# Attention steps of a fused attention, soft-MoE and FFN kernel: TensorE takes scores, values and router products together and then all transposes, and the copy of transposed x follows the exponential

## The chip, the cores and the metric

The kernel runs on one core of a Trainium2 chip. The metric is the device time of one execution in microseconds, lower is better. The engines are TensorE (PE in the rows, its weight loads PEld), VectorE (DVE), ScalarE (ACT), GpSimd (POOL) and SyncE (SP), which issues all the DMAs of this kernel.

## The reference

Three stages run one after the other: chunked attention with eight memory keys for each head, a soft mixture of experts, and a feed-forward block with a squared relu. Batch 4, 8 heads, 768 positions, head width 64; chunks of 32 queries see 16 keys to the left and 8 to the right.

```python
for c in range(nc):                                   # attention, 24 chunks of 32
    scores = scale * (q_c @ k_full.T)                 # k_full: 8 memory keys + up to 56 context keys
    a = exp(scores - max); a = a / (a.sum(-1) + 1e-9)
    out[:, :, c_start:c_end] = a @ v_full
x = out.transpose(0, 2, 1, 3).reshape(3072, 512)

logits = x @ phi                                      # soft MoE, 8 experts of 4 slots
d = softmax(logits, axis=0); slot_input = d.T @ x
slot_out[e] = relu(slot_input[e] @ w1[e]) @ w2[e]     # w1: 512 x 1024, w2: 1024 x 512
x = softmax(logits, axis=1) @ slot_out

h = relu(x @ w_in); out = (s * h * h + b) @ w_out     # FFN, 512 -> 2048 -> 512
```

## The kernel before

The attention is cut into 32 units (u = 0 to 31): four batches, two halves of 384 positions, four pairs of heads. Four units of one batch and half make a group g (0 to 7). A loop of 32 steps (s = 0 to 31) is a software pipeline written out by hand: each call in it is `when(unit, function)` or `at(s, k, function)`, and the order of the calls is the order of instructions on each engine, since nothing is rescheduled. The engines take their instructions in that order.

In step s the main work is this:

- `kspread(s+1)` on GpSimd spreads the keys of the next unit (lines L263 to L267).
- `emit_s(s)` on TensorE makes the scores (24 small matmuls, L285, and a mask, L288 or L290), into PSUM tile s. I write S(s).
- `soft_sum(s-1)`, `soft_max(s)`, `soft_eps(s-1)`, `soft_sub(s)`, `soft_rec(s-1)` on VectorE are the softmax's reductions, and `soft_exp(s)` on ScalarE is the exponential (L301).
- `emit_t(s-1)` transposes the exponentials on TensorE (L317, tile pt), and ScalarE copies them out of PSUM (L319). I write T(s-1).
- `emit_pv(s-2)` multiplies by the values (24 small matmuls, L325, tile x); VectorE evacuates and normalises them (`emit_xevac`, L331). I write PV(s-2).
- `emit_xt(s-3)` transposes the attention output on TensorE (L339, tile xt), and ScalarE copies that (L341 before, L344 in the changed file). I write xt(s-3).

Router work comes once for a group of four steps: `emit_lp` (L346, its copy `emit_g1` L351) in steps where s mod 4 is 3, `emit_g2` (L356, copy L358) and `emit_ln` (L362) where it is 0, `emit_g3` (L413, copy L414) where it is 1, and `emit_g4` (L419, slot inputs) where it is 2. After the loop an epilogue written out by hand drains the pipeline (units 30 and 31, group 7), and then come experts (L630 first weights, L668 second weights) and the FFN.

SyncE's queue takes the loads in program order. At the end of a step stand `load_qk(s+5)` (396 KB, into a ring of five buffers, free again after S of an older unit), in odd steps from 3 on `load_v(s+1)` (four DMAs of 192 KB, values of two units, into a ring of two buffers, free after PV of the older pair), and in odd steps one `load_w` (1 MB of expert weights). A DMA also waits for the DMA eight issues before it. After the loop the rest of the weights follow; where they reuse slots, they wait for the work on the old content.

Of the kernel before, what the change touches and what calls it, by code (L numbers as in the profile page):

```python
# [35 lines left out]
def kernel(  # L36
# [11 lines left out]
    nc = tc.nc  # L48
# [18 lines left out]
    def psum(tag, shape):  # L67
        bufs = {"s": 2, "g": 2}.get(tag, 1)
        return ps.tile(shape, F32, tag=tag, name=tag, bufs=bufs)
# [48 lines left out]
    with tc.manual_schedule():  # L118
# [27 lines left out]
        xts_r = Ring(p_r.end, 5, UT)  # L146
# [44 lines left out]
        def load_w(n, cap=None):  # L191
            for _ in range(n):
                i = wnext[0]
                if i < (len(order) if cap is None else cap):
                    src = srcs[order[i][0]][order[i][1]]
                    p = at_[order[i]] if i < npre else (16 + (i - npre) % NRG) * SLOT
                    if p is SPLIT:
                        wt[order[i]] = [area(x, SLOT // 2) for x in p]
                        for x in range(2):
                            nc.sync.dma_start(out=wt[order[i]][x], in_=src[:, SLOT // 2 * x:SLOT // 2 * (x + 1)])  # L200
                        wnext[0] += 1
                        continue
                    t = area(p, SLOT)
                    if order[i] == ("w2", W2 - 1):
                        wt[order[i]] = [t[:, SLOT // 2 * x:SLOT // 2 * (x + 1)] for x in range(2)]
                        for x in range(2):
                            nc.sync.dma_start(out=wt[order[i]][x], in_=src[:, SLOT // 2 * x:SLOT // 2 * (x + 1)])
                        wnext[0] += 1
                        continue
                    if src.dtype != F32:  # L210
                        t, src = t.bitcast(I32), src.bitcast(I32)
                    nc.sync.dma_start(out=t, in_=src)
                    wt[order[i]] = t
                    wnext[0] += 1
# [19 lines left out]
        def unit(u):  # L234
            g, hp = divmod(u, NHP)
            b, hf = divmod(g, HALF)
            return g, b, hf, hp
# [28 lines left out]
                                    in0=memk[:, b, hp].unsqueeze(2).to_broadcast([128, 2, NCU, NM]), **one)  # L266
            (nc.gpsimd if u else nc.vector).tensor_scalar(out=k[64:128, PAD + KL:], in0=k[64:128, PAD:PAD + UT], **one)  # L267

        s_t, x_t, gs = ({} for _ in range(3))

        def kwin(kt, c):
            a = kt[:, 32 * c:32 * c + KW]
# [38 lines left out]
        def soft_rec(u):  # L311
            nc.vector.reciprocal(out=r_r[u], in_=r_r[u])  # L312
# [8 lines left out]
        def emit_pv(u):  # L321
            xp = psum("s" if u == NU - 1 else "x", [128, NTU, 2, 64])
            for c in range(NCU):
                t, r = divmod(c, 4)
                nc.tensor.matmul(out=xp[32 * r:32 * r + 32, t], lhsT=pts_r[u][:, 32 * c:32 * c + 32],  # L325
                                 rhs=vbuf[u // 2 % 2][:, u % 2, :, 64 * c:64 * c + 64], start=True, stop=True)
            x_t[u] = xp

        def emit_xevac(u):
            g, b, hf, hp = unit(u)  # L330
            nc.vector.tensor_tensor(  # L331
                out=xs_r[g][:, :, 128 * hp:128 * hp + 128].rearrange("p t (h d) -> p t h d", h=2),
                in0=x_t.pop(u), in1=r_r[u].unsqueeze(3).to_broadcast([128, NTU, 2, 64]), op=ALU.mult)

        def emit_xt(u):
            g, b, hf, hp = unit(u)
            xt = psum("pt" if u == NU - 1 else "xt", [128, UT])
            for t in range(NTU):
                nc.tensor.transpose(out=xt[:, 128 * t:128 * t + 128],  # L339
                                    in_=xs_r[g][:, t, 128 * hp:128 * hp + 128], identity=ident)  # L340
            nc.scalar.copy(out=xts_r[u], in_=xt)  # L341

        def emit_lp(g):
            lp = psum("lp", [128, UT])  # L344
            for hp in range(NHP):
                nc.tensor.matmul(out=lp[32 * hp:32 * hp + 32, :], lhsT=phis[:, hp, :], rhs=xts_r[NHP * g + hp],  # L346
                                 start=True, stop=True)
            gs[g, "lp"] = lp
# [16 lines left out]
        def gsm(g):  # L365
            return [gsm_r[g][0:96, i:i + 1] for i in range(4)]
# [14 lines left out]
        def emit_ce(g):  # L381
            nc.scalar.activation(out=cs_r[g], in_=cs_r[g], func=AF.Exp)
# [7 lines left out]
        def emit_g2e(g):  # L390
            mo = mrun[(g + 1) % 2]
            gm, nmx, al, sg = gsm(g)
            nc.scalar.activation(out=eT_r[g][0:96], in_=lts_r[g][0:96], func=AF.Exp, bias=nmx,
                                 accum_out=lrun[0] if g == 0 else sg)
            if g:
                nc.scalar.activation(out=al, in_=mo, func=AF.Exp, bias=nmx)
            if g < NG - 1:
                emit_ce(g)
# [12 lines left out]
        def emit_g3(g):  # L411
            ep = psum("g", [128, NTU, NS])
            nc.tensor.transpose(out=ep.rearrange("p t s -> p (t s)"), in_=eT_r[g][0:96], identity=ident[0:96, 0:96])  # L413
            nc.scalar.copy(out=en_r[g], in_=ep)  # L414
# [36 lines left out]
        def at(s, k, *fns):  # L451
            if (s - k) % NHP == 0 and 0 <= (s - k) // NHP < NG:
                for fn in fns:
                    fn((s - k) // NHP)

        def when(u, fn):
            if 0 <= u < NU:
                fn(u)

        kspread(0)  # L460
        for s in range(NU):
            when(s + 1, kspread)
            at(s, 9, emit_g2e)
            when(s, emit_s)
            when(s - 1, soft_sum)
            when(s - 1, emit_t)
            at(s, 7, emit_lp)
            at(s, 8, emit_g2)
            at(s, 10, emit_g4)
            when(s, soft_max)  # L470
            when(s - 1, soft_eps)
            when(s, soft_sub)
            when(s, soft_exp)
            when(s - 1, soft_rec)
            at(s, 7, emit_g1)
            at(s, 10, emit_g4b)
            when(s - 2, emit_pv)
            at(s, 9, emit_g2b)
            when(s - 2, emit_xevac)
            at(s, 9, emit_g2c)  # L480
            at(s, 8, emit_ln)
            when(s - 3, emit_xt)
            at(s, 8, emit_g2a, emit_g2n)
            at(s, 9, emit_g3)
            when(s + NKB, load_qk)
            if s >= 3:
                when(s + 1, load_v)
            if s % 2 == 1:
                load_w(1, NWA)
            if s == NU - 2:  # L490
                load_w(1)
        load_w(19 - wnext[0])

        z, gl = NU - 1, NG - 1
# [29 lines left out]
        emit_xevac(z - 1)  # L524
        soft_rec(z)
        emit_xt(z - 2)
        emit_g2e(gl - 1)
        emit_pv(z)
        load_w(2)
        emit_xevac(z)  # L530
        emit_xt(z - 1)
        emit_xt(z)
        emit_g3(gl - 1)
        emit_lp(gl)
        load_w(1)
# [403 lines left out]
        for k in range(2):  # L939
# [3 lines left out]
                  in_=sot[:, k:k + 1, :, 0:4].to_broadcast([128, 4, 4, 4]))  # L943
# [151 lines left out]
```

## Time and profile before

| what | value |
|---|---|
| median of three runs | 471.84 us (471.58 to 471.96) |
| the profiled execution's own time | 473.56 us |
| its span | 471.8 us |
| PE busy | 453.8 us, 96% |
| PEld, DVE, ACT, POOL busy | 342.3, 309.8, 307.4, 84.2 us |
| DMA | 83.04 MB, mean 176 GB/s |

Busy time is summed over stages of different kinds: attention lasts until about 117 us of the span, the experts until about 167 us, and the rest is the FFN. A busy TensorE here is one whose matmuls, with modelled ends, overlap; it is not one at its peak. The DMA mean hides that nearly all loads fall in the first 172 us.

### The profile page before, as it was taken

What the parts mean: (1) busy time and instruction counts of PE and PEld (TensorE: products, weight loads), DVE (VectorE), ACT (ScalarE), POOL (GpSimd) and SP (SyncE); (2) the same over time, 40 slices, a digit from 0 to 9 for tenths busy, and PEclk for the clock granted to TensorE, in tenths of its full rate; (3) what the DMA queues carried; (4) which work ended last, traced back from release to release, by engine and by line L of the source; (5) the groups of instructions that cost most, each with busy time, mean ns of one, the idle gap of its engine ahead of it and who ended that gap; (6) DMA issues with size and microseconds to landing.
All of it is one profiled execution on the core that took longest, in us unless ns stands there. A gap on an engine that the chain in (4) does not pass through costs nothing.

```text
span 471.8 us, 10205 instructions
## 1 busy us (share of the span) xinstructions
PE 453.8 (96%) x3960; PEld 342.3 (73%) x3960; DVE 309.8 (66%) x685; ACT 307.4 (65%) x635; POOL 84.2 (18%) x154
## 2 busy tenths in 40 slices
PE   6898999899999989999999999999999999999996
PEld 5565767575555466878787888888888888888885
DVE  6677888876486879999495999976523224224232
ACT  4465766666224458898685988666666666666660
POOL 6665556541000000000000000007600000000000
PEclk8899999999999999999999999999999999999999
DMA  8999999999999952433422000004001001001011
GB/s 313 374 400 391 387 407 401 408 382 345 419 410 401 414 232 89 151 119 110 158 90 90 1 1 0 1 0 169 35 0 68 0 1 67 0 1 67 1 67 67
DMA packets 20576, 83.04 MB, mean 176 GB/s; under 512 B 2736, under 2 KB 2864, under 8 KB 14640
## 3 DMA queue, kind: packets, MB, share of 16 engines
q1 hardware_dynamic: 20528, 82.39, 45.1%
q8 instruction: 31, 0.51, 0.4%
q14 instruction: 17, 0.14, 0.1%
HBM read 76.09 MB, written 6.29 MB: 175 GB/s over the span
## 4 chain that ended last, share of the span: by engine, by line
PE 70%; DVE 11%; DMA 9%; ACT 3%; issue 2%; SPq 2%; POOL 1%; DVEq 0%; POOLq 0%; ACTq 0%
PE g L879 11%; PE xt L879 6%; PE x L879 6%; PE pt L879 5%; PE lp L879 5%; PE g L891 5%; DMA vals<-in_vm_dram 4%; PE s L827 4%; DMA seg<-in_w_dram 4%; PE x L325 3%; PE s L630 3%; PE xt L891 3%; PE x L891 3%; PE lp L891 3%; PE pt L891 3%
## 5 line engine op out<-in xcount | busy, mean ns | idle before, releaser
L844 DVE TENSOR_TENSOR glo<-r,ghi 128x384 fp32r<-128x384 f32 x128 | 76.5, 602 | 79.5 <-ACT ghi L841 79.3
L833 ACT ACTIVATE r<-s 128x384 f32<-128x384 f32 x128 | 62.7, 490 | 48.7 <-PE s L827 48.6
L837 ACT ACTIVATE r<-r 128x384 f32<-128x384 f32 x128 | 67.3, 526 | 9.6 <-DVE glo L844 5.4
L841 ACT CAST ghi<-r 128x384 fp32r<-128x384 f32 x128 | 65.4, 511 | 3.4
L827 PE MATMUL s<-cpack,mpack 128*128 128x384 f32 x128 | 44.3, 349 | 0.2 <-DVE mpack L820 0.2
L301 ACT ACTIVATE seg<-seg 128x384 f32<-128x384 f32 x32 | 28.7, 898 | 18.4 <-DVE seg L312 15.0
L879 PE MATMUL g<-whi,ghi 128*128 128x512 f32 x126 | 39.8, 395 | 0.2 <-DVE mpack L820 0.2
L891 PE MATMUL g<-wlo,ghi 128*128 128x512 f32 x128 | 39.7, 390 | 0.0
L879 PE MATMUL g<-whi,glo 128*128 128x512 f32 x126 | 39.3, 393 | 0.0
L866 POOL TENSOR_TENSOR keys<-keys,bias 128x512 f32<-128x512 f32 x6 | 8.4, 1428 | 162.6 <-DVE bias L855 162.6
L263 POOL TENSOR_SCALAR keys<-keys 64x416 f32<-64x416 f32 x63 | 33.6, 534 | 14.3 <-DMA keys<-in_kq_dram 9.0
L285 PE MATMUL s<-keys 128*32 128x128 f32 x768 | 30.1, 290 | 4.5 <-POOL keys L267 3.5
L325 PE MATMUL x<-vals,seg 128*32 128x128 f32 x744 | 28.5, 280 | 3.7 <-DMA vals<-in_vm_dram 2.9
L325 PEld LDWEIGHTS x<-vals,seg 128*32 128x32 f32 x744 | 20.7, 111 | 14.3 <-DVE seg L309 5.1
L827 PEld LDWEIGHTS s<-cpack,mpack 128*128 128x128 f32 x128 | 23.9, 188 | 7.7 <-issue 1.5
L891 PEld LDWEIGHTS g<-wlo,ghi 128*128 128x128 f32 x128 | 24.0, 188 | 5.1
L879 PEld LDWEIGHTS g<-whi,glo 128*128 128x128 f32 x126 | 23.6, 188 | 5.5
L319 ACT COPY seg<-pt 128x384 f32<-128x384 f32 x32 | 15.2, 475 | 18.5 <-PE pt L317 17.6
L285 PEld LDWEIGHTS s<-keys 128*32 128x32 f32 x768 | 19.4, 113 | 10.2 <-POOL keys L267 5.6
L879 PEld LDWEIGHTS g<-whi,ghi 128*128 128x128 f32 x126 | 23.7, 188 | 3.9 <-DVE mpack L820 0.7
L879 PE MATMUL pt<-whi,ghi 128*128 128x512 f32 x64 | 25.4, 397 | 0.2 <-DVE part L898 0.2
L879 PE MATMUL xt<-whi,ghi 128*128 128x512 f32 x64 | 25.5, 398 | 0.0
(255 smaller groups left out, 988.6 us busy)
## 6 DMA issues: line engine op xcount, KB each, us to landing
seg<-in_w_dram SPq DMA_DIRECT2D x27, 1024.0 KB, 8.6
keys<-in_kq_dram SPq DMA_DIRECT2D x32, 396.0 KB, 7.4
vals<-in_vm_dram SPq DMA_DIRECT2D x64, 192.0 KB, 6.5
keys<-in_w_in_dram SPq DMA_DIRECT2D x5, 1024.0 KB, 5.0
keys<-in_w_out_dram SPq DMA_DIRECT2D x5, 1024.0 KB, 5.1
out_dram<-os SPq DMA_DIRECT2D x18, 256.0 KB, 2.0
vals<-in_w_in_dram SPq DMA_DIRECT2D x3, 1024.0 KB, 6.2
vals<-in_w_out_dram SPq DMA_DIRECT2D x3, 1024.0 KB, 5.1
```

What stands on the lines that cost most here:

```text
L263: (nc.vector if h and u == 0 else nc.gpsimd).tensor_scalar(out=stream(kz[rows, h], 0, CH), in0=k[rows, UT * h:UT * h + (NCU + 1) * CH].rea ...
L285: nc.tensor.matmul(out=o, lhsT=qt[:, 32 * c:32 * c + 32], rhs=kz[:, :, at:at + WIN], start=True, stop=not (first or last))
L301: nc.scalar.activation(out=p_r[u], in_=sm_r[u].rearrange("p t h (a r) -> p t r (h a)", a=2), func=AF.Exp, scale=scale)
L319: nc.scalar.copy(out=pts_r[u], in_=pt)
L325: nc.tensor.matmul(out=xp[32 * r:32 * r + 32, t], lhsT=pts_r[u][:, 32 * c:32 * c + 32], rhs=vbuf[u // 2 % 2][:, u % 2, :, 64 * c:64 * c + ...
L827: nc.tensor.matmul(out=hq, lhsT=mpack[:, 128 * f:128 * f + 128], rhs=cpack[:, b * UT:(b + 1) * UT], start=True, stop=True)
L833: nc.scalar.activation(out=r_g[n % 2], in_=h_t.pop(n), func=AF.Relu)
L837: nc.scalar.activation(out=r2_g[n % 2], in_=r_g[n % 2], func=AF.Square)
L841: nc.scalar.copy(out=ghi_g[n % (LA + 2)], in_=r2_g[n % 2])
L844: nc.vector.tensor_tensor(out=glo_g[n % (LA + 2)], in0=r2_g[n % 2], in1=ghi_g[n % (LA + 2)].bitcast(F32), op=ALU.subtract)
L879: nc.tensor.matmul(out=o_t[r_][t], lhsT=gt[:, 128 * t:128 * t + 128], rhs=w_hi[f], start=(f == r_[1] and gt is ghi), stop=False)
L891: nc.tensor.matmul(out=o, lhsT=ghi[:, 128 * t:128 * t + 128], rhs=w_lo[f], start=False, stop=(f == f1 - 1))
```

## The change

In each step PV(s-2) and the router's matmuls `emit_lp`, `emit_g2`, `emit_g4` stand right behind S(s), and T(s-1), xt(s-3) and `emit_ln` behind those. `emit_xt` no longer issues its copy; a new function `emit_xc` does, and in the loop it stands behind `soft_exp(s)`. In the epilogue each `emit_xc` directly follows its `emit_xt`, as the copy did before. No instruction is added, removed or changed in shape.

```diff
-            nc.scalar.copy(out=xts_r[u], in_=xt)
+            xt_t[u] = xt
+
+        def emit_xc(u):
+            nc.scalar.copy(out=xts_r[u], in_=xt_t.pop(u))
...
             when(s, emit_s)
-            when(s - 1, soft_sum)
-            when(s - 1, emit_t)
+            when(s - 2, emit_pv)
             at(s, 7, emit_lp)
             at(s, 8, emit_g2)
             at(s, 10, emit_g4)
+            when(s - 1, soft_sum)
+            when(s - 1, emit_t)
+            when(s - 3, emit_xt)
+            at(s, 8, emit_ln)
             when(s, soft_max)
             when(s - 1, soft_eps)
             when(s, soft_sub)
             when(s, soft_exp)
+            when(s - 3, emit_xc)
             when(s - 1, soft_rec)
             at(s, 7, emit_g1)
             at(s, 10, emit_g4b)
-            when(s - 2, emit_pv)
             at(s, 9, emit_g2b)
             when(s - 2, emit_xevac)
             at(s, 9, emit_g2c)
-            at(s, 8, emit_ln)
-            when(s - 3, emit_xt)
             at(s, 8, emit_g2a, emit_g2n)
```

TensorE in step 26 (a step with `emit_g4`), before. The tiles s, pt, g, x and xt are PSUM tiles; seg_100 and seg_101 are SBUF areas that hold the small rings; vals_103 is one of the two value buffers.

```order
L285 MATMUL s<-keys 32x128 x11
L317 MATMUL pt<-ident,seg_100 128x128 x3
L419 MATMUL g<-seg_100,seg_101 32x512 x3
L325 MATMUL x<-vals_103,seg_100 32x128 x12
L339 MATMUL xt<-ident,seg_101 128x128 x3
```

The same step of the changed kernel (L422 is L419 of before):

```order
L285 MATMUL s<-keys 32x128 x11
L325 MATMUL x<-vals_103,seg_100 32x128 x12
L422 MATMUL g<-seg_100,seg_101 32x512 x3
L317 MATMUL pt<-ident,seg_100 128x128 x3
L339 MATMUL xt<-ident,seg_101 128x128 x3
```

What waited behind T(25) and g4, the product with the values that SyncE loads, now stands ahead of both.

ScalarE from the last step of the loop (s = 31) into the epilogue, before: copy of T(30), exponential of unit 31, copy of lp, copy of xt(28), copy of T(31), copy of g2.

```order
L319 COPY seg_100<-pt 128x384
L301 ACTIVATE seg_100<-seg_100 128x384
L351 COPY seg_100<-lp 128x384
L341 COPY seg_100<-xt 128x384
L319 COPY seg_100<-pt 128x384
L358 COPY seg_101<-g 96x128
```

The same place of the changed kernel (L344, L354 and L361 are L341, L351 and L358 of before):

```order
L319 COPY seg_100<-pt 128x384
L301 ACTIVATE seg_100<-seg_100 128x384
L344 COPY seg_100<-xt 128x384
L354 COPY seg_100<-lp 128x384
L319 COPY seg_100<-pt 128x384
L361 COPY seg_101<-g 96x128
```

On ScalarE the copies of xt and lp change places and the exponential stays behind the copy of T(30); on TensorE that T(30) now stands behind PV(29) and lp. VectorE's and GpSimd's orders are the same in both kernels.

## Rows read from the trace of the kernel before

**Rows 1.** The page's DMA issues: KB each, median us from issue to landing.

```profile
seg<-in_w_dram SPq DMA_DIRECT2D x27, 1024.0 KB, 8.6
keys<-in_kq_dram SPq DMA_DIRECT2D x32, 396.0 KB, 7.4
vals<-in_vm_dram SPq DMA_DIRECT2D x64, 192.0 KB, 6.5
```

**Rows 2.** Chain that ended last: start us, length us, what; a wait for values.

```profile
86.42 7.68 DMA vals<-in_vm_dram
```

**Rows 3.** Windows of four us: stretch, length, granted clock share, DMA share, GB/s.

```profile
92.00:96.00 4.00, 1.00 1.00 402
...
108.00:112.00 4.00, 1.00 0.90 300
...
144.00:148.00 4.00, 1.00 0.98 367
```

**Rows 4.** Chain that ended last, from the epilogue to the second expert weights.

```profile
112.85 0.29 DVE seg L371
...
145.33 0.33 SPq L212
...
149.21 16.58 DMA seg<-in_w_dram
...
165.83 0.64 PE xt L668 x8
```

**Rows 5.** TensorE's timeline, steps 26 to 27: start, length, line, tile, idle before.

```profile
91.85 1.06 PE L419 MATMUL g<-seg,seg 128*32 128x512 f32 x6
94.23 0.86 PE L325 MATMUL x<-vals,seg 128*32 128x128 f32 x24 [1.32 <-DMA vals<-in_vm_dram]
95.03 0.55 PE L339 MATMUL xt<-ident,seg 128*128 128x128 f32 x3
95.50 0.43 PE L285 MATMUL s<-keys 128*32 128x128 f32 x8
...
96.34 0.55 PE L317 MATMUL pt<-ident,seg 128*128 128x128 f32 x3
96.82 0.85 PE L346 MATMUL lp<-seg,cstt 128*32 128x384 f32 x8
97.49 0.84 PE L325 MATMUL x<-vals,seg 128*32 128x128 f32 x24
98.26 0.55 PE L339 MATMUL xt<-ident,seg 128*128 128x128 f32 x3
```

**Rows 6.** TensorE's timeline, steps 28 to 31.

```profile
98.73 0.86 PE L285 MATMUL s<-keys 128*32 128x128 f32 x24
99.43 0.21 PE L290 MATMUL s<-maskt,sel 128*32 128x16 f32 x2
...
100.67 0.86 PE L325 MATMUL x<-vals,seg 128*32 128x128 f32 x24 [0.20 <-DVE seg L309]
...
105.81 0.55 PE L317 MATMUL pt<-ident,seg 128*128 128x128 f32 x3 [0.20 <-ACT seg L301]
...
108.44 0.86 PE L285 MATMUL s<-keys 128*32 128x128 f32 x24
```

**Rows 7.** ScalarE's timeline, end of the loop and start of the epilogue.

```profile
109.86 0.48 ACT L319 COPY seg<-pt 128x384 f32<-128x384 f32 x1 [0.84 <-PE pt L317]
110.65 0.89 ACT L301 ACTIVATE seg<-seg 128x384 f32<-128x384 f32 x1 [0.31 <-DVE seg L312]
111.44 0.46 ACT L351 COPY seg<-lp 128x384 f32<-128x384 f32 x1
111.80 0.48 ACT L341 COPY seg<-xt 128x384 f32<-128x384 f32 x1
112.18 0.49 ACT L319 COPY seg<-pt 128x384 f32<-128x384 f32 x1
112.55 0.27 ACT L358 COPY seg<-g 96x128 f32<-96x128 f32 x1
```

More of the change, by code (lines that the diff above doesn't have):

```diff
@@ L267, in kspread @@
             (nc.gpsimd if u else nc.vector).tensor_scalar(out=k[64:128, PAD + KL:], in0=k[64:128, PAD:PAD + UT], **one)
-        s_t, x_t, gs = ({} for _ in range(3))
+        s_t, x_t, xt_t, gs = ({} for _ in range(4))
         def kwin(kt, c):
@@ L526 @@
         emit_xt(z - 2)
+        emit_xc(z - 2)
         emit_g2e(gl - 1)
@@ L531 @@
         emit_xt(z - 1)
+        emit_xc(z - 1)
         emit_xt(z)
+        emit_xc(z)
         emit_g3(gl - 1)
```

## The prediction

> **What bounds the kernel now.** I first read the windows of four microseconds for the DMA, because the change sits in a stage in which all engines are busy and only one of them can be the bound. From the first microseconds to about 100 us the loads run without a gap: at 92 to 96 us the DMA share is 1.00 at 402 GB/s [rows 3]. Two steps of the loop load two units of queries and keys, the values of two units and one expert weight, 2 x 396 + 4 x 192 + 1024 = 2584 KB, or 2.65 MB [rows 1]. At 402 GB/s that is 6.6 us, 3.3 us for a step. Reordering TensorE cannot make these bytes come sooner. The chain of waits shows the same thing from the other side: TensorE waits for the values of unit 24, whose last DMA was issued at 86.42 us and took 7.68 us [rows 2], and PV(24) starts only at 94.23 us after 1.32 us of idle time [rows 5].
>
> Near the end of the attention the bound changes. At 108 to 112 us the DMA moves only 300 GB/s [rows 3], because the next loads need slots that the attention still holds. Then the chain goes through the engines: the last exponential, the copies on ScalarE, VectorE's first reduction of the epilogue at 112.85 us, the experts, and SyncE, which at 145.33 us issues expert weights whose slots have just come free; the last of them is issued at 149.21 us and lands 16.58 us later, where TensorE at 165.83 us is waiting [rows 4]. At 144 to 148 us the DMA fell to 367 GB/s [rows 3], so its queue had run dry when those weights were issued. A later end of the attention is therefore passed on one for one to 165.83 us, and to the end of the kernel, since the FFN behind it is a fixed sequence. So the question is how far the change shifts the epilogue's start.
>
> **The change, part by part.** No instruction is added. Three things move.
>
> First, PV(s-2) now stands ahead of the router's matmuls and of T(s-1). Where PV waits for values, that work is no longer done during the wait but behind it. In step 26 before, T(25) and g4 were already issued when the wait began; from PV(24) to the next scores took 95.50 - 94.23 = 1.27 us. After: PV .80 us (94.23 to 95.03), g4 1.06 us (its length), T .48 us (96.34 to 96.82), xt .47 us (95.03 to 95.50), together 2.81 us [rows 5]. If the values land when they did, S(27) is 1.54 us later. The lower bound comes from the landing: 7.68 us is 1.18 us above the 6.5 us median of the value loads [rows 1, 2]. The loads are issued in the same order behind a full queue, so they land neither much sooner nor later on average, but this one may have been a late one. With a median landing the shift is .36 us. I see nothing that decides between these two and take the middle, **+.95 us**, with both ends kept.
>
> Second, from S(27) to S(31) TensorE took 108.44 - 95.50 = 12.94 us [rows 5, 6]. In it stand a wait of PV for VectorE (.20 us at 100.67) and one of T for the exponential (.20 us at 105.81) [rows 6]. Both go: PV now needs an evacuation made a whole step earlier, and T stands a PV later, when the exponential is done. Also 24 narrow matmuls (128\*32) took .70 us in S, with another narrow one behind them (98.73 to 99.43) [rows 6], but .77 us in PV, with a 128\*128 transpose behind (97.49 to 98.26) [rows 5]. I read the .07 us as the price of going from narrow to wide. Before, a step went wide twice, behind S and behind PV; now it does so once. Four steps save .28 us. A new wait stands against this: the copy of lp now stands behind the exponential and the copy of xt on ScalarE, so that g2 in step 28 finds it about .2 us late. (The exponential begins 3.21 us after the scores, as worked out below; the exponential and the copy of xt take .79 and .36 us on ScalarE [rows 7], the copy of lp .46 us: 4.82 us. TensorE is at g2 after a step of 3.23 us less .14 us, and S and PV of .84 and .77 us less .07 us: 4.63 us.) Sum: -.4 - .28 + .2, about **-.5 us**, between -.3 and -.7.
>
> The Trainium skill (page "TensorEngine Tiling (Array Packing)", section "Tiling Modes", under its key properties) says that changing the tiling mode, not just the tile, drains TensorE. The trace agrees in kind with .07 us between the two groups of 24 [rows 5, 6]; the page gives no price, so a sum by it has the sign of the term above and no other size.
>
> Third, in the last step the exponential. ScalarE takes its work in order: copy of T(30) at 109.86 us, exponential of unit 31 at 110.65 us, which waited only for VectorE [rows 7]. That is 2.21 us after S(31) began at 108.44 us [rows 6]. Now T(30) stands behind PV(29) and lp, and the exponential still behind the copy of T(30): S .84 us (95.50 to 96.34), PV .77 us, lp .67 us (96.82 to 97.49), T .55 us (its length) [rows 5], one copy .38 us (111.80 to 112.18) [rows 7], together 3.21 us. So the exponential of unit 31, for which T(31) and the whole epilogue wait, begins **+1.0 us** later against S(31). In earlier steps the same delay of the exponential is hidden, because T(s) comes a whole step of some 3.2 us later; here there is no next step to hide it. What is queued behind it on ScalarE, copies of xt(28), lp, T(31) and g2, is late with it, and VectorE's L371 waits for the last of these.
>
> Behind the exponential the copy of xt now goes before that of lp. Before, lp's copy began at 111.44 us, right behind the exponential; now it begins a copy later, .38 us. g2 needs it, and VectorE's reduction at 112.85 us needs g2's copy [rows 4, 7]. Before, g2 waited for T(31) on TensorE rather than for lp, so some of the .38 us is slack: **+.2 us**, between 0 and .38.
>
> SyncE's queue keeps its order. `load_v` waits for PV, which now directly follows S, so it is free to issue sooner within a step; with the DMA at 402 GB/s and full share [rows 3] that is worth nothing while the queue is full.
>
> Sum: .95 - .5 + 1.0 + .2 = 1.65 us; its ends are .36 - .7 + 1.0 + 0 = .66 and 1.54 - .3 + 1.0 + .38 = 2.62 us. The profiled execution took 473.56 us, so it would take 475.2 us; it stands 1.72 us above the median of 471.84 us. On the median the forecast is **473.5 us**, own range 472.5 to 474.5 us.
>
> **The rivals.** A difference of .2%, .94 us, is about what a measurement of this kernel can tell from no change.
>
> *Hidden.* The epilogue begins later, but its end is paced by bytes and the shift is swallowed. It needs a DMA queue that does not run dry at 144 us, if the later attention also leaves more loads in flight. The 367 GB/s there [rows 3] speaks against it; that the queue is full in all the windows around it speaks for it. Or the landing of step 26 is early and the sum comes out at its lower end. Time 471.5 to 472.7 us, chance .26.
>
> *Faster.* TensorE, not the loads, paces the steps. Then .07 us in each of 32 steps and two waits of .20 us in each of eight groups of four, 2.2 + 3.2 = 5.4 us, are gained, less the 1.2 us of the end: 467.6 us at best. For it: TensorE is busy almost without a gap, and the two waits and the narrow-to-wide step are in the rows [rows 5, 6]. Against it: 2.65 MB in two steps at 402 GB/s are 6.6 us whatever TensorE does [rows 1, 3]. It decides from the point where the values of step 26 land 3.2 us sooner than before and TensorE is there to take them: 1.54 - 3.2 - .5 + 1.2 = -.96 us, 470.9 us. This is also where the page's rule on draining would lead, if TensorE were the bound. Chance .10.
>
> *Slower still.* The new wait of g2 for the copy of lp, in each of eight groups, and the later exponential, for which VectorE's sum of the next step waits, lengthen the steps so much that TensorE falls behind the loads. With .5 us a group instead of .2 that is 8 x .3 = 2.4 us on top of 1.65 us, 475.9 us at worst. For it: ScalarE and VectorE each have a chain through the exponential in every step, with only .31 us of waiting in front of it in step 31 [rows 7]. Against it: a step has 3.3 us by the loads and needs less on every engine. Chance .10.
>
> That the change does not do what it says is excluded, since both orders are shown above.
>
> **How the numbers follow.** The forecast's own case has .54, and nearly all of it lies above +.94 us (.50); with the slower rival that makes .60 for slower. The hidden case and the rest of the forecast's give .29 for same, and the faster case, with a little of the hidden one, .11. The range holds the forecast's case and most of the hidden one, 471.5 to 474.8 us; left out are most of faster and most of slower still, together under .2.
>
> **What would show it right or wrong.** In the changed kernel's profile: PV of an even unit in a step with g4 waits for a value DMA, and g4 and T follow it (right), or no such wait is left (then the first term is wrong, and the faster rival gains). From S(27) to S(31) 12.3 to 12.7 us. The exponential of unit 31 begins about 3.2 us after S(31) and directly behind the copy of T(30). L371 of the epilogue comes 1.65 us later than 112.85 us, and the last expert weight and the end of the span later by as much; if L371 is late but the weight is not, the hidden rival is right. What would make the prediction wrong above all is another landing pattern of the value loads, since its first term is a middle of two bounds.

## Result and the profile after

The changed kernel took 475.59 us (median of six runs, 474.15 to 478.37); the kernel before, run beside it, 472.30 us (six runs). The ratio is 1.0061 with a 95% interval of 1.0037 to 1.0085: slower by 1.8 to 4.0 us. (The ratios, here and below, are estimated from the single runs and are not the quotients of the medians, 1.0070 here.) The direction is the one forecast, the size is not: 473.5 us was forecast, and the range ended at 474.8. One of all the runs below, 485.00 us with PV alone moved, was in the chip's slower state and is left out. The profiled execution took 474.83 us with a span of 473.0.

TensorE's timeline of the changed kernel, PV(21) and then steps 26 and 27 (start, length, line, tile, idle time before and what ended it), answers to [rows 5]:

```profile
83.15 0.30 PE L325 MATMUL x<-vals,seg 128*32 128x128 f32 x3
...
91.01 0.43 PE L285 MATMUL s<-keys 128*32 128x128 f32 x8
...
92.91 0.86 PE L325 MATMUL x<-vals,seg 128*32 128x128 f32 x24 [1.00 <-ACT seg L417]
93.56 1.06 PE L422 MATMUL g<-seg,seg 128*32 128x512 f32 x6
94.56 0.55 PE L317 MATMUL pt<-ident,seg 128*128 128x128 f32 x3
94.94 0.49 PE L339 MATMUL xt<-ident,seg 128*128 128x128 f32 x3
95.36 0.43 PE L285 MATMUL s<-keys 128*32 128x128 f32 x8
```

PV(24) waits 1.00 us and g4, T(25) and xt come behind the wait, as forecast. Between PV(24) and S(27) there are now 95.36 - 92.91 = 2.45 us where there were 1.27 [rows 5]. But PV(24) itself came 1.32 us sooner than in the profile before, so S(27) is not later here at all. The name in brackets misleads: L417 is the copy that g4 needs, not PV. What PV waits for is seen from SyncE, in the answer for the tile of values between 82 and 90 us (issues with their own length in ns and first and last start; then us from issue to landing):

```profile
L251 SPq DMA_DIRECT2D vals<-in_vm_dram x4: 599/602/605, 84.5 to 86.5; - x4
...
DMA to landing us min/median/max: 6.3/6.6/6.8
```

The last of the four value loads is issued at 86.5 us and lands 6.3 to 6.8 us later, 92.8 to 93.3: that is when PV(24) begins. The four are issued behind PV(21), which frees their buffer (its start is 83.15 us), so the way from PV(21) to PV(24) is a round trip of 9.76 us. In the kernel before it took 11.23 us, and 10.13 in its second profile further below: the new order does not make this way longer.

The chain that ended last, from the end of the attention to the second expert weights (start us, length us, what), answers to [rows 4, 6, 7]:

```profile
107.98 0.86 PE s L285 x24
...
108.89 0.67 PE x L325 x21
109.56 0.65 PE lp L349 x8
110.21 0.49 PE pt L317 x3
...
110.72 0.02 ACT seg L319
110.75 0.35 issue
111.10 0.86 ACT seg L301
111.96 0.37 ACT seg L344
112.33 0.39 ACT seg L354
...
112.76 0.45 PE g L359 x6
...
113.24 0.27 ACT seg L361
...
113.53 0.29 DVE seg L374
...
146.04 0.33 SPq L212
...
150.26 16.76 DMA seg<-in_w_dram
...
167.06 0.64 PE xt L675 x8
```

Here the reader can follow the forecast's third part piece by piece: S(31), PV(29), lp, T(30), the copy of T(30) (from 110.72 us; the chain counts most of it as "issue"), and only then the exponential, 111.10 - 107.98 = 3.12 us behind S(31); before, 2.21 [rows 6, 7]. Then the copies of xt and lp, g2, its copy, and VectorE's first reduction of the epilogue at 113.53 us, 2.43 us behind the exponential (before 2.20 [rows 4, 7]). From S(31) to the epilogue: 5.55 us, before 4.41.

In the last three rows SyncE comes to the freed slots .71 us later than before (146.04 against 145.33 [rows 4]), the epilogue being .68 us later; the last weight is used 1.23 us later. The windows of four microseconds show what happens to the queue in the meantime (stretch, length, granted clock, DMA share, GB/s):

```profile
108.00:112.00 4.00, 1.00 0.98 372
128.00:132.00 4.00, 1.00 0.68 223
144.00:148.00 4.00, 1.00 0.78 283
```

At 108 to 112 us more is moved than before (372 against 300 GB/s [rows 3]), but the queue then runs dry twice while SyncE waits for slots: 223 GB/s at 128 to 132 us, where the kernel before moved 410:

```profile
128.00:132.00 4.00, 1.00 1.01 410
```

and 283 against 367 GB/s at 144 to 148 us [rows 3]. So what the attention loses at its end isn't absorbed by the loads.

In this pair of profiles S(31) is .46 us earlier (107.98 against 108.44 [rows 6]), the tail 1.14 us longer and the end of the span 1.2 us later, while the medians are 3.3 us apart. One profile of each doesn't show the loop's share, and that became the question of the experiments.

### The profile page after: what moved, and what is told of

The parts are those of the page before. It is cut to its first block, busy times and chain, and to the rows that moved or that the text cites. A ratio compares the mean times of both kernels' runs of the same rounds, so it can differ in the third digit from the quotient of the medians.

```text
span 473.0 us, 10209 instructions
## 1 busy us (share of the span) xinstructions
PE 447.1 (95%) x3960; PEld 342.5 (72%) x3960; DVE 307.3 (65%) x685; ACT 304.9 (64%) x635; POOL 84.1 (18%) x154
## 4 chain that ended last, share of the span: by engine, by line
PE 66%; DMA 11%; DVE 11%; ACT 4%; issue 3%; SPq 2%; POOL 2%; DVEq 0%; POOLq 0%; ACTq 0%
PE g L886 11%; PE xt L886 6%; PE x L886 5%; PE pt L886 5%; PE lp L886 5%; PE g L898 5%; DMA vals<-in_vm_dram 4%; PE s L834 4%; DMA seg<-in_w_dram 4%; PE s L637 3%; DMA keys<-in_kq_dram 3%; PE xt L898 3%; PE x L898 3%; PE lp L898 3%; PE pt L898 3%
## 5 line engine op out<-in xcount | busy, mean ns | idle before, releaser
L325 PEld LDWEIGHTS x<-vals,seg 128*32 128x32 f32 x744 | 21.9, 112 | 11.0 <-ACT seg L417 5.9
L305 DVE TENSOR_REDUCE seg<-seg 128x6 f32<-128x384 f32 x32 | 17.8, 555 | 16.5 <-ACT seg L301 16.2
```

The lines of the kernel that those rows point to most:

```text
L305: nc.vector.tensor_reduce(out=r_r[u], in_=p_r[u].rearrange("p t r (h a) -> p t h r a", h=2), axis=AX.XY, op=ALU.add)
```

## Experiments

"The order before" is the order of instructions in the loop's body before the change, "the new order" that of the change. The kernel before ran beside each group, on the same chip: medians of 472.69 us (first group), 473.09 (second), 472.98 (third), 472.92 (fourth) and 472.89 (fifth), 11 to 25 runs each. The steps of the loop (u, s) are counted as ahead of the prediction.

### First group: the tail or the loop

Theory T: the loss is made in step 31, where the exponential comes later. Theory L: it is made in the loop.

**The changed kernel again**, no edit.

> The changed kernel once more. Theory T (the tail): the last step's exponential stands behind PV(29), lp and T(30), the epilogue is late by about .7 us, and the rest of the loss is lost load time behind it; span 1 to 2 us above that of before, and in the profile S(31) begins no later than before while the exponential of unit 31 begins about 3.1 us after S(31). Theory L (the loop): the values that PV waits for land in another pattern from execution to execution, and the steps with g4 then stand still with g4 and T behind; S(31) then is later than 108.44 us by up to 1.5 us in some executions, and the time is 2 to 4 us above before.

Measured: 475.31 us (474.69 to 476.71), ratio 1.0055 (1.0038 to 1.0073). The epilogue began at 115.63 us in this profile, 2.1 us later than in the first. The difference arises in step 10. TensorE's timeline there:

```profile
40.10 0.60 PE L325 MATMUL x<-vals,seg 128*32 128x128 f32 x11 [1.24 <-DMA vals<-in_vm_dram]
41.22 0.81 PE L325 MATMUL x<-vals,seg 128*32 128x128 f32 x11 [0.52 <-issue]
...
42.02 1.92 PE L422 MATMUL g<-seg,seg 128*32 128x512 f32 x4
43.87 0.90 PE L317 MATMUL pt<-ident,seg 128*128 128x128 f32 x3
...
45.08 0.43 PE L285 MATMUL s<-keys 128*32 128x128 f32 x8
```

and the windows of one microsecond (length, PE busy and instructions, granted clock, DMA share, GB/s):

```profile
40.00:41.00 1.00, 0.60 (x11) 1.00 0.97 385
41.00:42.00 1.00, 0.78 (x15) 0.66 1.00 393
42.00:43.00 1.00, 1.00 (x10) 0.50 1.04 399
43.00:44.00 1.00, 1.00 (x5) 0.50 1.11 406
44.00:45.00 1.00, 1.00 (x6) 0.63 1.03 400
```

PV(8) waited for its values, stood once more in its middle, and then the granted clock went from 1.00 to .50 (from 2.4 to 1.2 GHz) for some 3 us, just when g4 and T(9) ran: T took .90 us instead of .55. The first profile of this kernel has the same two stands of PV(8), without a fall:

```profile
40.94 0.53 PE L325 MATMUL x<-vals,seg 128*32 128x128 f32 x11 [0.61 <-issue]
...
43.16 0.43 PE L285 MATMUL s<-keys 128*32 128x128 f32 x8
```

From the end of the second stand to S(11) it takes 2.22 us there and 45.08 - 41.22 = 3.86 here: the fall costs 1.64 us in this step.

**The order before, with step 31 in the new order**, and **the new order, with step 31 in the order before**.

```diff
+            if s == NU - 1:        # the second kernel: if s < NU - 1
+                (new order)
+            else:
+                (order before)
```

> The order of before in steps 0 to 30 and the changed order in step 31 alone. Theory T: nearly the whole loss is here, +1.0 to +2.0 us on before, the exponential of unit 31 about 3.1 us after S(31) instead of 2.2. Theory L: only the tail's part, +.7 us or less, no measurable loss.

> The changed order in steps 0 to 30 and the order of before in step 31. Theory T: the loss is gone, within .5 us of before or a little faster (S(31) came .46 us sooner in the changed kernel's profile). Theory L: still 1.5 us or more slower than before.

Measured: 473.65 us, 1.0017 (1.0003 to 1.0032), and 474.94 us, 1.0050 (1.0031 to 1.0069). Step 31 alone costs .1 to 1.5 us; the loop alone 1.5 to 3.3, by the medians the larger share. The two are not clean halves: in the second kernel the exponential of unit 30 is still late, T(30) waits .21 us for it in step 31, and from S(31) to the epilogue it is 5.00 us, .59 more than before.

**PV alone moved**, T, the router's matmuls, xt and the copies where they were.

```diff
             when(s, emit_s)
+            when(s - 2, emit_pv)
...
-            when(s - 2, emit_pv)
```

> The order of before with PV(s-2) alone moved behind S(s); T, router work and xt with its copy stay in their order. Here T(30) in the last step stands behind PV but still ahead of lp, so the exponential of unit 31 is late by about .77 - .3 = .4 us instead of .9. Theory T: +.3 to +.8 us. Theory L: PV's waits for values stand ahead of T and g4 as in the changed kernel, so the loss is the changed kernel's, 1.5 us or more.

Measured: 481.86 us (477.61 to 483.95), 1.0160 (1.0123 to 1.0198), much worse than the whole change. In steps with g4 TensorE stands in the middle of PV, with nothing that the profile shows to wait for:

```profile
53.26 0.63 PE L325 MATMUL x<-vals,seg 128*32 128x128 f32 x13 [0.34 <-DMA vals<-in_vm_dram]
55.17 0.63 PE L325 MATMUL x<-vals,seg 128*32 128x128 f32 x11 [1.28 <-issue]
```

So this kernel doesn't isolate one part of the change; it has a disturbance of its own: six such stops, 7.4 us together, five of them in steps with g4. The last section shows what they are.

### Second group: which part of the loop

Theory W: PV's wait in the steps with g4 holds back g4 and T. Theory O: another part of the order costs, in every step.

**The new order, T and g4 ahead of PV in the steps with g4.**

```diff
+            g4s = s >= 10 and s % 4 == 2
+            if g4s:
+                when(s - 1, soft_sum)
+                when(s - 1, emit_t)
+                at(s, 10, emit_g4)
             when(s - 2, emit_pv)
```

> The changed order, but in the seven steps with g4 T(s-1) and g4 stand ahead of PV(s-2) as before. Theory W (the wait of PV for values holds back T and g4 behind it, and in a bad execution TensorE stands so long that its clock falls): most of the loop's loss goes, at most +1.2 us on before (the tail's part). Theory O (the loop's loss comes from another part of the order, the early xt or the exponential behind the copy of T in every step): still +2 us or more.

Measured: 475.69 us, 1.0060 (1.0037 to 1.0084), as slow as the changed kernel. W in its simple form fails. The profile says why the undoing doesn't pay: from PV(24) to S(27) it is 2.17 us, little less than 2.45, and S(27) to S(31) is 13.18 us, .54 longer. T, ahead of PV again, now waits for the exponential, which the new order makes late: T(25) .40 us, T(29) .37 us. And in step 28 PV stands .25 us in its middle without a releaser.

**The order before, steps with g4 in the new order.**

```diff
+            if s >= 10 and s % 4 == 2:
+                (new order)
+            else:
+                (order before)
```

> The order of before, and only the seven steps with g4 in the changed order. Theory W: nearly the loop's whole loss appears, +1.5 us or more on before. Theory O: +.5 us or less.

Measured: 474.96 us, 1.0039 (1.0024 to 1.0054). These steps alone bring 1.1 to 2.6 us, as W said.

**No expert weight loaded during the steps**, in both orders; the weights are loaded behind the loop instead.

```diff
-            if s % 2 == 1:
-                load_w(1, NWA)
-            if s == NU - 2:
-                load_w(1)
```

> The changed order without the sixteen loads of expert weights inside the loop; they are all loaded after it, so that the kernel as a whole is longer and is compared with the next one. In the loop the DMA then has 1.6 instead of 2.65 MB in two steps. Theory W: PV no longer waits for values, S(31) begins several us sooner than 108 us and not later than in the next kernel; the two kernels differ by the tail alone, .5 to 1.2 us. Theory O: this one stays 2 us or more behind the next one.

> The order of before without the loads of expert weights inside the loop. The partner of the kernel before this one. S(31) at 100 to 104 us by what its steps take without waits for loads.

Measured: 501.31 us (new order) and 502.04 us (order before); the loads behind the loop now set the end. The loop is what counts: S(11) to S(31) takes 102.90 - 40.00 = 62.90 us in the new order and 103.72 - 40.84 = 62.88 in the one before. O is refuted: without the weights' bytes the new order isn't slower. It isn't faster either, since TensorE finds a new wait in every fourth step, here step 30 of the new order:

```profile
100.20 0.86 PE L325 MATMUL x<-vals,seg 128*32 128x128 f32 x24 [0.51 <-ACT seg L301]
```

VectorE's timeline of that kernel shows its cause:

```profile
99.56 0.55 DVE L331 TENSOR_TENSOR seg<-x,seg 128x384 f32<-128x384 f32 x1
```

That is the evacuation of x, which has one PSUM buffer. It ends at 100.11 us and PV starts .09 us behind it. PV has come so early that the buffer isn't free.

### Third group: the value loads' round trip

Theory V: the loop's loss comes of the values, which are let go by PV(u-3) and waited for by PV(u), with the rest of the step behind. Theory A: the order itself costs, above all the exponential behind the copy of T.

**A third buffer for the values**, loaded two steps further ahead, in both orders. It takes two of the slots that are loaded during the steps.

```diff
-                when(s + 1, load_v)
+                when(s + 3, load_v)
...
-                load_w(1, NWA)
+                load_w(1, NWA - 2)
```

> The old order with a third buffer for the values, loaded two steps further ahead (it stands where two of the fifteen expert weights were loaded during the steps; those two, 2 MB, come after step 31). It is the base for the next run, not for the kernel before. Theory V (in the changed kernel PV stands and waits for a value load with everything else of the step behind it) and theory A (the order itself costs: the product g2 behind the copy of lp, the exponential behind the copy of T, PV behind the release of its one PSUM buffer): the same here. The DMA waits of PV should be gone; since the loads are what paces the steps, the end is expected between 470 and 476 us.

> The changed order with the same third buffer. Theory V: no PV waits for values any more, so only the step 31 part is left of the loss: 0.7 to 1.3 us above the run with the old order and the third buffer. Theory A: the loss of the loop stays: 2.5 to 3.2 us above it. Both: S(31) and the waits of PV in the profile show which.

Measured: 491.80 and 491.67 us. In this pair an expert weight was loaded into the buffer that PV(30) and PV(31) still read, so these two products are computed from weights, and they wait for that load; the end says nothing of the theories. The loop does: no PV waits for values, and S(31) begins at 107.11 us in the new order, 107.57 in the one before.

**The new order, copy of T behind the exponential.**

```diff
             when(s, soft_exp)
+            when(s - 1, emit_tc)     # the copy, no longer in emit_t
```

> The changed order, but the copy of the transposed probabilities stands behind the exponential of the step's unit on ScalarE, in every step. In step 31 this puts exp(31) ahead of the copy of T(30). Theory V: takes back only the step 31 part, 0.7 to 1.0 us of the 2.6 to 2.9: 1.8 to 2.0 us above the kernel before. Theory A, if the exponential behind that copy is what costs in every step: 0 to 0.5 us above the kernel before. A third outcome, above the changed kernel, if PV then waits for the later copy.

Measured: 475.68 us, 1.0056 (1.0039 to 1.0074): nothing is gained, and A falls in the form stated. ScalarE's timeline of this kernel in step 31:

```profile
111.29 0.86 ACT L301 ACTIVATE seg<-seg 128x384 f32<-128x384 f32 x1 [1.75 <-PE pt L317]
112.05 0.46 ACT L322 COPY seg<-pt 128x384 f32<-128x384 f32 x1
```

The exponential now waits for T(30) itself: it writes the one buffer of probabilities that T(30) reads. It starts 3.23 us behind S(31) (108.06), no earlier than in the changed kernel. My expectation had left out this buffer; the copy stood in the way only as the second of two.

**The kernel before again**, no edit.

> The kernel before once more, for a second profile: how far S(11), S(27), S(31) and the last expert weight move between executions of one kernel. Theory V: S(31) between 106.5 and 108.5 us and the last weight landing 52.5 to 53.2 us behind the last step of the attention; the changed kernel's S(31) 1 to 2 us later on average. Theory A: the same here.

Measured: 475.22 us in that execution, with S(31) at 107.84 us and the epilogue at 112.27, both *earlier* than in [rows 4, 6]. TensorE's timeline:

```profile
93.64 0.86 PE L325 MATMUL x<-vals,seg 128*32 128x128 f32 x24 [0.29 <-DMA vals<-in_vm_dram]
94.43 0.55 PE L339 MATMUL xt<-ident,seg 128*128 128x128 f32 x3
94.91 0.43 PE L285 MATMUL s<-keys 128*32 128x128 f32 x8
```

From the epilogue to the end of the span this execution took 361.1 us, that of [rows 4] 359.0. So the last loads scatter by 2 us from one execution to the next, whatever the attention does.

### Fourth group: the third buffer, mended

The buffers are numbered so that the last values lie where no weight comes early; all of the reference is computed.

```diff
-vbuf[u // 2 % 3]
+vbuf[(u // 2 + 1) % 3]
```

> The old order with a third value buffer, loaded two steps further ahead; two of the fifteen expert weights loaded during the steps come after step 29 instead. It computes the whole reference. Base for the next run. The bytes are the same, so the steps stay at 13.2 us per four; end between 471.5 and 475 us.

> The changed order with the same third buffer. Theory V (round trip of the value loads): no wait for values is left, S(27) and S(31) are not later than with the old order (the first pair showed S(31) .46 us earlier), and only the 1.1 us from S(31) to the epilogue are: 0.4 to 1.1 us above the old order with the third buffer. Rival (the order itself): 2.4 to 3 us above it.

Measured: 473.18 us, 1.0006 (.9987 to 1.0024), in the order before, and 474.44 us, 1.0030 (1.0015 to 1.0044), in the new one. The two are 1.26 us apart; the changed kernel and the kernel before, 2.3 to 3.3. TensorE's timeline of the new order with three buffers, S(27) and the PV(24) ahead of it:

```profile
92.40 0.86 PE L328 MATMUL x<-vals,seg 128*32 128x128 f32 x24 [0.49 <-ACT seg L304]
...
95.22 0.44 PE L288 MATMUL s<-keys 128*32 128x128 f32 x8 [0.30 <-POOL keys L270]
```

and of the order before:

```profile
93.74 0.41 PE L328 MATMUL x<-vals,seg 128*32 128x128 f32 x2
...
95.65 0.44 PE L288 MATMUL s<-keys 128*32 128x128 f32 x8
```

PV's remaining wait is the PSUM buffer's. S(27) is earlier in the new order, S(31) too (108.14 against 108.56 us). VectorE's first reduction of the epilogue, new order and order before:

```profile
113.69 0.28 DVE L377 TENSOR_REDUCE seg<-seg 96x1 f32<-96x128 f32 x1 [0.99 <-ACT seg L364]
```

```profile
112.98 0.28 DVE L377 TENSOR_REDUCE seg<-seg 96x1 f32<-96x128 f32 x1 [0.51 <-ACT seg L364]
```

113.69 - 108.14 = 5.55 us and 112.98 - 108.56 = 4.42: the tail is as long as without the third buffer, and in this pair it is all that is left of the loss. So the pair, one profile each, agrees with V; its expectation of .4 to 1.1 us was a little low.

**The new order, T(25) and g4 ahead of PV(24) in step 26 alone** (the diff of the second group, with `s == 26`).

> The changed order, only in step 26 T(25) and g4 stand ahead of PV(24) as before. Theory V in the form of the prediction's first term (the last late value load decides): S(27) begins about 1.3 us behind PV(24) instead of 2.45, and the time is 1.0 to 1.5 us below the changed kernel, 1.3 to 1.9 above the kernel before. Rival, theory V as a sum over many steps, or the order itself: 0 to 0.5 us below the changed kernel.

Measured: 475.62 us, 1.0061 (1.0039 to 1.0083), no gain. The profile, at 478.72 us the slowest of its runs, doesn't settle it: a clock fall in step 22 had put PV(24) at 95.03 us, where its values were there already; T(25) ahead of it had waited .51 us for the exponential; and in step 30 g4 stood in its middle without a releaser:

```profile
107.62 1.05 PE L422 MATMUL g<-seg 128*32 128x512 f32 x4
109.11 1.02 PE L422 MATMUL g<-seg 128*32 128x512 f32 x2 [0.44 <-issue]
```

**The changed kernel, a third profile.**

> The changed kernel once more, for a third profile. Theory V: PV(24) begins about 9.8 us behind PV(21), 2.45 us ahead of S(27); S(31) 12.6 us behind S(27); the epilogue 5.55 us behind S(31). The rival leaves these open.

Measured: 475.91 us in this execution; 9.78 us from PV(21) to PV(24), 2.45 us to S(27), 12.62 to S(31), 5.54 to the epilogue at 114.18 us. All four lengths are as expected. In step 6 PV(4) had waited 2.26 us, and the clock had fallen to .50 behind it.

### Fifth group: the clock

Theory C: the falls of the granted clock are part of the loop's loss. If so, work for TensorE during PV's wait should keep the clock up and make the kernel faster.

**The new order with ten filler matmuls ahead of PV** in the steps with g4; they compute nothing of the reference.

```diff
+            if s >= 6 and s % 4 == 2:
+                warm(10)
             when(s - 2, emit_pv)
```

> The changed order with ten matmuls (each 128 by 256 of output, bf16, about 1.07 us together at full clock) that compute nothing of the reference ahead of PV in each step with g4 from step 6 on, so that TensorE works while PV's values are on their way. [...] Rival (the clock falls are too rare or their loss is taken back by the loads): the same as the changed kernel within 0.3 us, or above it by the fillers that find no wait (up to 0.5 us).

> The changed kernel, beside the filled one on the same chip: 475.3 to 475.7 us median. Theory C: of its profiles some 3 in 7 show the fall. The rival: the same, without a tie to the time.

Measured: 476.17 us (473.94 to 478.17), 1.0064 (1.0041 to 1.0087), and for the changed kernel beside it 475.16 us (474.25 to 476.27), 1.0049 (1.0032 to 1.0067). Neither profile has a fall behind 20 us, so they compare nothing on the clock. The fillers make nothing faster, and a share of the clock isn't shown. How much of a fall's 1.64 us (first group) reaches the end stays open: the two profiled executions of the changed kernel with a fall took 476.26 and 475.91 us, the two without 474.83 and 474.63.

## Why the prediction was wrong

What failed are sizes, not the path: the base of 471.84 us was .5 to 1.25 us too low, the term of PV ahead of g4 and T was +1.18 us and not +.95, and the gain from S(27) to S(31) was .29 us and not .5, because of a wait that the prediction had left out. Together they account for .8 to 1.4 us of the 1.7 to 2.1 us by which 473.5 us was too low; the rest is not settled.

All profiles together give what one could not. From the timelines of TensorE and VectorE, in us:

```
kernel                            PV(24)  to S(27)  S(27)-S(31)  S(31)-epilogue   sum    against before
before                             94.23    1.27      12.94          4.41        18.62
before, again                      93.64    1.27      12.93          4.43        18.63
before, step 31 new                92.72    1.27      12.93          5.55        19.75     +1.13
before, steps with g4 new          92.84    2.44      12.84          4.77        20.05     +1.43
changed                            92.91    2.45      12.62          5.55        20.62     +2.00
changed, again                     94.98    2.45      12.65          5.55        20.65     +2.03
changed, third                     93.57    2.45      12.62          5.54        20.61     +1.99
changed, fourth                    92.73    2.45      12.66          5.56        20.67     +2.05
new, step 31 as before             92.05    2.45      12.84          5.00        20.29     +1.67
new, T and g4 ahead of PV          93.73    2.17      13.18          5.55        20.90     +2.28
new, copy of T behind exponential  92.56    2.44      13.06          6.04        21.54     +2.92
new, filled                        92.45    2.44      13.08          5.65        21.17     +2.55
new, T and g4 ahead, step 26 only  95.03    1.91      13.93          5.66        21.50     +2.88
```

PV(24) starts when its values land, in both orders alike: 93.53 us on average over the first three profiles, 93.55 over the four of the changed kernel. With single values from 92.7 to 95.0 us, that the two agree so closely is luck; a shift of half a microsecond would not show. What follows it is fixed to .05 us within a kernel. The last column, the later start of the epilogue if PV(24) starts at the same time, lies inside the measured interval of every one of these kernels (step 31 new: +.1 to 1.5 us; steps with g4 new: 1.1 to 2.6; changed, three times: 1.8 to 4.0, 1.8 to 3.5, 1.5 to 3.2; step 31 as before: 1.5 to 3.3; T and g4 ahead: 1.8 to 4.0; copy behind: 1.8 to 3.5; filled: 1.9 to 4.1; step 26 only: 1.8 to 3.9). That is a weak test, since these intervals are 1.4 to 2.4 us wide: in the three measurements of the changed kernel the column lies .9, .6 and .3 us below the middle. The kernel with PV alone moved does not fit (+4.7 us by the same lengths, measured 5.8 to 9.4); its PV(24) itself came at 98.49 us.

Now the forecast's steps, one by one.

*PV ahead of g4 and T, "+.95 us"*: the mechanism was right, the size failed. I took the middle between 1.54 us (values land as they did) and .36 (they land a median's time). The runs show no shift of the landings, so the upper end was the right case; but its sum of four rows, 2.81 us from PV(24) to S(27), was too long by .36: PV to g4 took .65 us, not .80, g4 to T 1.00, not 1.06, T to xt .38, not .48, and xt to S .42, not .47. T and xt now follow each other in one tiling. The Trainium skill (page "TensorEngine Tiling (Array Packing)", section "Tiling Modes") has the change of mode drain TensorE; the .10 us by which T became shorter agree. The shift is 2.45 - 1.27 = +1.18 us.

*S(27) to S(31), "about -.5 us"*: -.29 us (12.64 on average against 12.93), within the 12.3 to 12.7 us that were to show it right. What was wrong is that both waits go: PV's wait for VectorE comes back in step 30 as one for the PSUM buffer of x, .42 to .44 us in all four profiles of the changed kernel. In the first of them TensorE's and VectorE's rows are:

```profile
105.29 0.86 PE L325 MATMUL x<-vals,seg 128*32 128x128 f32 x24 [0.42 <-ACT seg L301]
```

```profile
104.64 0.55 DVE L331 TENSOR_TENSOR seg<-x,seg 128x384 f32<-128x384 f32 x1
```

The evacuation of the unit before ends at 105.19 us, .10 us ahead of PV(28).

*The exponential of unit 31, "+1.0", and the copy of lp, "+.2"*: 3.12 - 2.21 = +.91 us and 2.43 - 2.20 = +.23. Right.

*One for one to the end*: right, within the 2 us by which single executions scatter. From the epilogue to the end of the span it took 359.0 and 361.1 us in the two profiles before, 359.5, 358.9, 359.9 and 359.5 in the four of the changed kernel, and 360.3 with PV alone moved, where the epilogue began at 121.84 us, 9 us later. The "hidden" rival is refuted by this and by the queue's dry stretches at 128 and 144 us.

The sum is +2.02 us instead of +1.65. The larger part of the miss is the base. The sum was set on the 471.84 us of three runs, which agreed within .4 us; with three more (472.65 to 474.99 us) the median was 472.30, in later groups 472.69 to 473.09. On 472.30 the measured terms give 474.3 us, on 472.69 and 472.89 474.7 and 474.9, against 475.59, 475.31 and 475.16. What is left, 1.3, .6 and .3 us, lies within the intervals; whether the clock falls or the breaks in TensorE's issue hold a part of it is not settled. (Falls in three of eight executions at 1.64 us each would be .6 us on average; that is an estimate from the two figures, not a measurement.) On the 473.56 us of the profiled execution the sum gave 475.2 us, close to what was measured; but that execution lay above every later median of the kernel before, so this is luck. And the range had no term for the scatter between executions: PV(24) alone moves by 2.3 us between the profiles of the changed kernel.

*The "faster" rival* (5.4 us, if TensorE paced the steps) was wrong in its price too: with the weights' loads gone, TensorE paces both orders at 62.9 us for 20 steps, and what the new order gains in the steps with u mod 4 = 3 and 1 (2.94 and 2.40 us instead of 3.23 and 2.67) it gives back in the other two (3.12 and 4.12 instead of 2.88 and 3.79), part of it to the PSUM buffer's wait. *"Slower still"* had the right time and the wrong mechanism, since the steps aren't longer.

None of the kernels beats the one before. The order before with three value buffers equals it (.9987 to 1.0024).

## What to carry to other kernels

Where a load is let go by one use and waited for by a later one, what stands behind the waiting instruction in program order is late by its full length, and what stands ahead of it is free: count from the landing, not from the step. At the end of a pipelined loop an instruction that moves behind others costs in full what in the middle the next iteration hides, and the buffer that it writes (here that of the probabilities, which T still reads) must be counted among its waits. Before a change of half a per cent is forecast, look at several runs of the kernel before: three that agree may still lie half a microsecond or a whole one below its median.

## What the runs showed of the hardware

In three of eight profiles in the new order, or nearly so, with two value buffers, the weights' loads and no fillers the granted clock fell from 1.00 to .50 behind 20 us, each time at a wait of PV (2.26 us in step 6; 1.24 and .52 us in step 10; 2.08 us in step 22), with TensorE busy up to it; with PV alone moved it fell at 27.5 us, behind a wait of 1.75 us. It stayed at .50 for about 3 us although TensorE was busy again, as the window rows of the first group show. The length of the wait alone doesn't decide it: a wait of 2.09 us at 69 us of the execution that fell in step 10 passed without a fall, and in two other profiles of the changed kernel PV(8) stood 1.21 and .61 us, and 1.18 and .54 us, also without one, where 1.24 and .52 us had been followed by one. In seven profiles of the order before, or of it with single steps in the new one, none fell between 20 us and the end of the loop.

TensorE also stops where the profile shows nothing to wait for, in the middle of a group of like matmuls: 1.28 us at 55.17 us and up to 1.84 us (at 70.15 us) with PV alone moved, .44 us in g4 above. The packed traces show where. Count TensorE's records (weight loads, matmuls, semaphore instructions) from the kernel's start, the first as 0: the matmuls behind these three stops have the numbers 1729, 2242 and 3777, 193 or 194 beyond a multiple of 256. The same holds for all 24 stops of .2 us or more that stand as "issue" between 20 and 120 us in the twenty profiles, whatever matmul is there; in three of four profiles of the changed kernel it is the same one, number 1217 in step 10 (.52 to .61 us). The page of the changed kernel lists, among the DMA queues (packets, MB, share):

```profile
q8 instruction: 31, 0.51, 0.4%
```

A packet of this queue has 16384 bytes, and there is one for some 256 of TensorE's 2 x 3960 instructions. Each of the 24 stops ends 1.2 to 1.7 us behind the end of such a packet (with PV alone moved, packets end at 53.59 and 68.64 us). So TensorE stood for its own instructions. The Trainium skill (page "Runtime: NRT & Kernel Launch", section "Instruction fetch mechanics") says that instructions are refilled in blocks of 256 and that this is mostly hidden. The traces agree on the blocks; in these 24 places the refill was not hidden. Without the weights' loads in the loop no such stop occurs there, in either order. That fits packets that come late behind full queues, but the kernel before, with full queues, has only one stop of .2 us in two profiles, so what makes a packet late isn't isolated.
